# Attention with landmark memories and a bilinear feed-forward: the softmax of four of eight batches moved onto token partitions

## The chip, the cores and the metric

The kernel runs on one core of a Trainium2 chip. The metric is the device time of one execution in microseconds (us), taken as the median of several executions. TensorE is called PE in the profile, its weight loads PEld, VectorE is DVE, ScalarE is ACT, GpSimd is POOL and SyncE is SP.

## The reference, cut to what matters

There are 8 batches, 8 heads, 576 tokens (S), a head size of 64 (D) and 32 memories per head (M). The feed-forward has 512 inputs and 1536 hidden units.

```python
a   = softmax(phi, axis=2)                  # over the tokens
k_m = einsum('bhsm,bhsd->bhmd', a, k)
v_m = einsum('bhsm,bhsd->bhmd', a, v)
scores = matmul(q, k_m.T) / sqrt(64)        # 576 x 32 per head
attn   = softmax(scores, axis=-1)           # over the 32 memories of a head
x   = matmul(attn, v_m)                     # then heads side by side: 4608 x 512
out = ((x @ w_a) * (x @ w_b)) @ w_out       # 4608 x 512
```

The second softmax, over the 32 memories, is what the change moves.

## The kernel before, in words

**The work of one batch.** `exp_phi` (ACT) gives the exponentials of phi. `kv_sums` (PE, tile `pkv`) sums keys, values and a column of ones over the tokens; `take_kv` (DVE) divides by the sum and lays the result out in `rep`; `rep` is transposed into `kvT`, either by PE and a DVE copy (`kv_transpose`, unit `kvt`) or by a DMA transpose that SP issues (`kv_turn`, unit `kvd`). `q_transpose` (DVE) turns the queries into `qT`. `scores` (unit `sc`) multiplies `kvT` and `qT` on PE into four PSUM banks `pscore`, with the 128 (head, memory) pairs of a group g on the partitions and tokens in the columns. `exp_scores` (ACT, L310) writes `E`.

**The normalisation before.** A sum over 32 memories is a sum over partitions there. `denominators` (L320, L321) therefore multiplies `E` by a block matrix `ones` on PE into `pD`, two matmuls of 288 columns per group, and takes the logarithm on ACT (`L`). `normalise` (L329, L331) takes `R` = exp(-L) on ACT and multiplies `E` by `R` into the attention tile `A`, on DVE in batches 0 and 1 and on POOL from batch 2.

**The feed-forward.** The value memories are folded into the weights: `fold` (unit `v0` to `v2`, L343) makes `vab`, one third of 512 hidden units at a time for w_a and w_b (two bodies z), in four PSUM banks `pva`; `take_fold` (units `x0a` and so on, L355) evicts them, group 0 on ACT and group 1 on DVE. `up_half` (L601, L609, L612) multiplies `vab` by `A` in halves of 288 tokens: `pa` is copied to `a_sb` by ACT, and DVE multiplies `a_sb` by `pb` into `ht`. The down projection runs over pairs of 128-token blocks with seven products in place of eight (`two_downs`, L473, tiles `py`, `pv`, `px`); it needs sums of blocks of `ht` that POOL makes (`h_sums`, L455), and its partial results are read by ACT (L480, L527) and DVE (L484).

**The order.** The program's order is written by hand. A batch from the third on has 24 steps (12 blocks of hidden units for each half of the tokens). After each step `work.advance()` issues some down products at an even rate, and then one slot of a side list runs; the side list prepares the next batch. A slot is a set of units joined by `+`; a name with `'` belongs to the batch after that one, `dN` pulls N down products, `L` issues the four loads of two batches later from POOL, `-` does nothing. The lists are `second` (beside batch 2, preparing 3), `every` (beside batches 3, 4 and 5, preparing 4, 5 and 6) and `last` (beside batch 6, preparing 7). Batch 2 is prepared beside the second half of batch 1, by the list `slots(2, ...)` at L699.

**PSUM.** The eight banks are dealt out in a fixed rotation by the class `Banks`: a bank goes to the end of the line when it is taken and again when it is freed. The rotation is decided when the program is written, so PE waits for the very bank that is next in line, even where another is empty. From batch 3 on `work.settle()` finishes the product under way before `sc` and before a pair of folds, so that only the bank of `py` stays held there.

Each engine runs its instructions in the program's order.

Of the kernel before, what the change touches and what calls it, by code (L numbers as in the profile page):

```python
# [8 lines left out]
F32 = mybir.dt.float32  # L9
F16 = mybir.dt.float16  # L10
AF = mybir.ActivationFunctionType
ALU = mybir.AluOpType

P = 128
# [4 lines left out]
def kernel(  # L19
# [11 lines left out]
    nc = tc.nc  # L31

    B, H, S, D = q.shape
    M = phi.shape[3]
# [11 lines left out]
    mid = ctx.enter_context(tc.tile_pool(name="mid", bufs=2))  # L46
    small = ctx.enter_context(tc.tile_pool(name="small", bufs=2))
# [28 lines left out]
    def load_phi(b):  # L76
        phis[b] = inp.tile([P, NHP, NI * M], F32, name="phi_sb")
        nc.gpsimd.dma_start(out=phis[b], in_=rows(phi, b))

    def load_k(b, hps=slice(0, NHP)):  # L80
        kvs[b] = kv_sbs[b % 2]
        nc.gpsimd.dma_start(out=kvs[b][:, 0, hps], in_=rows(k, b)[:, hps])

    def load_v(b, hps=slice(0, NHP)):
        nc.gpsimd.dma_start(out=kvs[b][:, 1, hps], in_=rows(v, b)[:, hps])

    def load_q(b, hps=slice(0, NHP)):
        if b not in qs:
            qs[b] = inp.tile([P, NHP, NI * D], F16, name="q_sb")
        nc.gpsimd.dma_start(out=qs[b][:, hps], in_=rows(q, b)[:, hps])  # L90

    def load(b):
        load_phi(b)
        load_k(b)
        load_v(b)
        load_q(b)
# [81 lines left out]
    attn = {}  # L178
# [7 lines left out]
    def units(b):  # L186

        u = {}
        t = {}
# [133 lines left out]
        def normalise(g, hfs=slice(0, 2)):  # L323
            if g == 0 and hfs.start == 0:
                attn[b] = mid.tile([P, 2, S], F16, name="A")
            sl = slice(HALF * hfs.start, HALF * hfs.stop)
            if hfs.start == 0:
                t["R", g] = small.tile([P, S], F16, name="R")
            nc.scalar.activation(out=t["R", g][:, sl], in_=t["L", g][:, sl], func=AF.Exp, scale=-1.0)  # L329
            engine = nc.vector if b < 2 else nc.gpsimd  # L330
            engine.tensor_tensor(out=attn[b][:, g, sl], in0=t["E"][:, g, sl], in1=t["R", g][:, sl], op=ALU.mult)  # L331

        def fold(lo, hi, zs):
            if b not in vabs:
                vabs[b] = [mid.tile([P, 2, d_ff], F16, name=f"vab{x}") for x in range(2)]
            if len(zs) > 1 and b > 2:
                work.settle()
            for z in zs:
                t["pva", lo, z] = [banks.take([P, 512], F32, "pva", hold=True) for _ in range(2)]
                for j in range(4):  # L340
                    for g in range(2):
                        r, hp = head(g, j)
                        nc.tensor.matmul(  # L343
                            t["pva", lo, z][g][0][32 * j:32 * j + 32, 0:hi - lo],
                            t["kvT"][64 * r:64 * r + 64, 4 + g, M * j:M * j + M],
                            w_sbs[z][64 * r:64 * r + 64, hp, lo:hi],
                            start=True,
                            stop=True,
                            tile_position=(64 * r, 32 * j),
                        )  # L350

        def take_fold(lo, hi, z):
            for g, engine_copy in enumerate((nc.scalar.copy, nc.vector.tensor_copy)):
                pva, bank = t["pva", lo, z][g]
                engine_copy(out=vabs[b][z][:, g, lo:hi], in_=pva[:, 0:hi - lo])  # L355
                banks.free(bank)

        def one(f, *a):
            return lambda: f(*a)

        for z in range(2):
            u[f"exp{z}"] = one(exp_phi, z)
            u[f"ks{z}"] = one(sums, z, 0)
            u[f"kt{z}"] = one(transpose, z, 0)
            u[f"vs{z}"] = one(sums, z, 1)
            u[f"vt{z}"] = one(transpose, z, 1)
            u[f"s{z}"] = one(scores, (z,))
            u[f"e{z}"] = one(exp_scores, z)
            u[f"km{z}"] = one(take_kv, (z,))
            u[f"den{z}"] = one(denominators, z)  # L370
            u[f"nr{z}"] = one(normalise, z)
            for hf in range(2):
                u[f"den{z}{hf}"] = one(denominators, z, (hf,))
                u[f"nr{z}{hf}"] = one(normalise, z, slice(hf, hf + 1))
            for n in range(NCH):
                u[f"v{n}{'ab'[z]}"] = one(fold, 512 * n, 512 * (n + 1), (z,))
                u[f"x{n}{'ab'[z]}"] = one(take_fold, 512 * n, 512 * (n + 1), z)
            for n in range(2):
                u[f"hv{n}{'ab'[z]}"] = one(fold, 256 * n, 256 * (n + 1), (z,))
                u[f"hx{n}{'ab'[z]}"] = one(take_fold, 256 * n, 256 * (n + 1), z)  # L380
# [6 lines left out]
        u["km"] = one(take_kv)  # L387
        u["kvt"] = one(kv_transpose)
        u["kvd"] = one(kv_turn)
        u["-"] = lambda: None  # L390
        return u

# [221 lines left out]
    def up(b, i, hfs):  # L614
        for hf in hfs:
            up_half(b, i, hf, 0)
        if len(hfs) > 1:
            yield
        for hf in hfs:
            up_half(b, i, hf, 1)  # L620
        yield

    def ups(steps, side=()):

        side = iter(side)
        for step in steps:
            for _ in up(*step):
                work.advance()
                next(side, us[step[0]]["-"])()
        for f in side:  # L630
            work.advance()
            f()

    def steps(b, lo, hi):

        return [(b, i, (0, 1)) for i in range(lo, hi)]

    def half_steps(b, hf, lo=0):

        return [(b, i, (hf,)) for i in range(lo, NFF)]  # L640

    us = {b: units(b) for b in range(B)}

    def named(b, names):
# [6 lines left out]
    def slots(b, names):  # L651

        def both(fs):
            return lambda: [f() for f in fs]
        def unit(n):
            if n == "fin":
                return lambda: work.pull(-work.done % NFF)
            if n == "L":
                return lambda: load(b + 2) if b + 2 < B else None
            if n[0] == "y":  # L660
                return lambda: some(int(n[1:]))
            if n[0] == "d" and n[1:].isdigit():
                return lambda: work.pull(int(n[1:]))
            return us[b + n.endswith("'") - n.endswith("_")][n.rstrip("'_")]

        return [both([unit(n) for n in x.split("+")]) for x in names.split()]
# [3 lines left out]
    def some(n):  # L670
        for _ in range(n):
            next(early, None)
# [21 lines left out]
    load(3)  # L694
    sum_weights()
    ups(steps(1, 0, 4), slots(1, "- y1+hv1a+hx1a hv1b+hx1b - y3+v1a+x1a y3+v1b+x1b - -"))
    ups(half_steps(1, 0, 4), slots(1, "- v2a+x2a+v2b+x2b+qt0' - - qt1'+exp0' exp1'+qt2' - kv'+km'+y9"))
    work.plan(S + HALF, 10)
    ups(half_steps(1, 1, 4), slots(2, "qt3 kvt - sc+e0+e1 - den0+den1+nr0 - v0+nr1+x0a x0b - v1+x1b x1a"))  # L699
    second = "v2_+d1+x2a_+exp0 x2b_ exp1 - kv+km+d2 qt0 d4+kvt+qt1 - qt2+qt3+sc+e0 - e1+v0+d2+x0a+x0b den0+d3 exp0' v1+nr0+x1a x1b+qt0' L+d5 den1 v2+x2a exp1'+qt1'+x2b - - qt2'+kv'+nr1+km' - - qt3'+kvt'+d5"  # L700
    every = "- sc+e0 e1 den0 nr0+v0+x0a+x0b - - exp0' exp1' - v1+x1b+x1a+kv'+km0'+d3 - den1+km1' kvd'+qt0' - - nr1+qt1' v2+x2a+x2b - qt2' - qt3' - - L"
    last = "sc+e0 d3 - e1 v0+x0b - - den1 - - den0+d1 x0a+v1+x1b x1a+nr0 - - - v2+x2a - nr1 - - - - x2b"
    for b in range(2, B):
        if b == 2:
            load(4)
        names = second if b == 2 else every if b + 2 < B else last
        side = slots(b + 1, names) if b + 1 < B else []
        for hf in range(2):
            work.plan(S * b + HALF * hf, NFF)
            ups(half_steps(b, hf), side[NFF * hf:NFF * (hf + 1)] if hf == 0 else side[NFF:])  # L710
# [30 lines left out]
```

The softmax here doesn't subtract the row's maximum and nothing guards it: scores larger than these inputs give would overflow.

## Time and profile before

| | |
|---|---|
| median of 5 runs | 241.35 us (241.06 to 241.97) |
| the profiled execution | 241.26 us, of which its span is 239.6 us |
| PE busy | 230.2 us, 96% of the span, 3092 matmuls |
| DVE, ACT, POOL busy | 165.4, 158.5 and 159.3 us |
| granted PE clock | 1.0 |
| normalisation on PE: `pD` | 32 matmuls of 288 columns, four per batch |
| `E`, `L`, `R` on ACT | 419 ns, 426 ns, 712 ns each |
| `A` on POOL | 12 of 1277 ns |
| fold evictions of 512 columns | 44 on ACT at 606 ns, 44 on DVE at 684 ns |
| DMA transposes of `rep` (6 blocks of 128 x 128) | 3, landed 2.7, 3.2 and 3.6 us after issue |

A row of the groups names the line, engine and operation, the tiles written and read, the shape, the count, the busy time and the mean of one. Matmuls overlap in the pipe, so a row's 286 ns for a 288-column matmul is not what the matmul costs; the distance between the starts of two rows in the timeline is.

### The profile page before, as it was taken

What the parts mean: (1) busy time and instruction counts of PE and PEld (TensorE: products, weight loads), DVE (VectorE), ACT (ScalarE), POOL (GpSimd) and SP (SyncE); (2) the same over time, 40 slices, a digit from 0 to 9 for tenths busy, and PEclk for the clock granted to TensorE, in tenths of its full rate; (3) what the DMA queues carried; (4) which work ended last, traced back from release to release, by engine and by line L of the source; (5) the groups of instructions that cost most, each with busy time, mean ns of one, the idle gap of its engine ahead of it and who ended that gap; (6) DMA issues with size and microseconds to landing.
All of it is one profiled execution on the core that took longest, in us unless ns stands there. A gap on an engine that the chain in (4) does not pass through costs nothing.

```text
span 239.6 us, 7764 instructions
## 1 busy us (share of the span) xinstructions
PE 230.2 (96%) x3092; PEld 170.0 (71%) x3092; DVE 165.4 (69%) x403; ACT 158.5 (66%) x410; POOL 159.3 (66%) x135
## 2 busy tenths in 40 slices
PE   7968999999999999999999999999999999999993
PEld 7634664446757867878787787878787778888882
DVE  4636783469949878976974659775976585756642
ACT  2267671669698599687776857697776877465330
POOL 7953244499979639981799948984769087936001
PEclk9999999999999999999999999999999999999999
DMA  6999999999967954992359945599230303032154
GB/s 237 238 195 206 207 258 205 254 211 280 223 151 164 208 118 97 228 204 48 47 120 232 211 91 68 150 199 193 45 81 15 77 19 72 11 82 63 39 129 122
DMA packets 28164, 34.71 MB, mean 145 GB/s; under 512 B 4416, under 2 KB 22208, under 8 KB 28128
## 3 DMA queue, kind: packets, MB, share of 16 engines
q0 software_dynamic: 19264, 23.14, 52.1%
q1 hardware_dynamic: 8352, 10.29, 18.2%
q10 hardware_dynamic: 512, 0.79, 1.0%
q8 instruction: 24, 0.39, 0.6%
q14 instruction: 12, 0.10, 0.1%
HBM read 42.47 MB, written 9.44 MB: 217 GB/s over the span
## 4 chain that ended last, share of the span: by engine, by line
PE 76%; DMA 16%; DVE 2%; ACT 2%; issue 1%; POOL 1%; DVEq 0%; POOLq 0%
PE py L473 18%; PE pa L601 17%; PE pb L601 16%; PE pv L473 9%; DMA wb_sb<-in_moe_w_b_dram 6%; DMA q_sb<-in_q_dram 5%; PE pva L343 5%; DMA kv_sb<-in_v_dram 4%; PE px L473 4%; PE po L398 2%; PE pkv L212 2%; PE pscore L297 1%; PE pD L320 1%; ACT a_sb L609 1%; DVE ht L612 1%
## 5 line engine op out<-in xcount | busy, mean ns | idle before, releaser
L612 DVE TENSOR_TENSOR ht<-a_sb,pb 128x288 f16<-128x288 f16 x168 | 73.2, 449 | 37.5 <-ACT a_sb L609 28.4
L601 PEld LDWEIGHTS <-vab 128*128 128x128 f16 x768 | 72.4, 98 | 25.0 <-issue 7.9
L609 ACT CAST a_sb<-pa 128x288 f16<-128x288 f32 x168 | 66.8, 408 | 25.8 <-PE pa L601 24.6
L601 PE MATMUL pa<-A,vab 128*128 128x288 f16 x384 | 75.8, 287 | 0.1
L601 PE MATMUL pb<-A,vab 128*128 128x288 f16 x384 | 74.9, 286 | 0.7 <-ACT vab L355 0.5
L455 POOL TENSOR_TENSOR h_sums<-ht 128x768 f16<-128x768 f16 x28 | 46.0, 1643 | 33.9 <-DVE ht L612 33.8
L473 PEld LDWEIGHTS <-h_sums 128*128 128x128 f16 x384 | 37.0, 98 | 7.7 <-issue 1.1
L355 DVE CAST vab<-pva 128x512 f16<-128x512 f32 (+1 forms) x52 | 32.3, 644 | 4.8 <-PE pva L343 4.2
L355 ACT CAST vab<-pva 128x512 f16<-128x512 f32 (+1 forms) x52 | 27.8, 572 | 7.8 <-PE pva L343 7.4
L473 PEld LDWEIGHTS <-ht 128*128 128x128 f16 x288 | 28.1, 98 | 5.7 <-issue 0.4
L473 PE MATMUL py<-w_sums,h_sums 128*128 128x256 f16 x192 | 31.3, 273 | 0.0
L455 POOL TENSOR_TENSOR h_sums<-h_sums,ht 128x768 f16<-128x768 f16 x14 | 22.9, 1639 | 1.0
L455 POOL TENSOR_TENSOR h_sums<-ht,h_sums 128x768 f16<-128x768 f16 x14 | 23.0, 1642 | 0.9
L310 ACT ACTIVATE E<-pscore 128x288 f16<-128x288 f32 x32 | 11.4, 419 | 11.5 <-PE pscore L297 11.4
L331 POOL TENSOR_TENSOR A<-E,R 128x576 f16<-128x576 f16 x12 | 15.3, 1277 | 4.3 <-ACT R L329 4.3
L473 PE MATMUL py<-wo_sb,ht 128*128 128x256 f16 x96 | 16.7, 273 | 0.0
L473 PE MATMUL pv<-w_sums,h_sums 128*128 128x256 f16 x96 | 16.5, 273 | 0.0
L473 PE MATMUL py<-w_sums,ht 128*128 128x256 f16 x96 | 15.9, 272 | 0.1
L473 PE MATMUL px<-wo_sb,ht 128*128 128x256 f16 x96 | 15.9, 273 | 0.0
L321 ACT ACTIVATE L<-pD 128x288 f32<-128x288 f32 x32 | 11.6, 426 | 5.8 <-PE pD L320 5.6
L480 ACT ACTIVATE u<-py 128x256 f32<-128x256 f32 x32 | 12.5, 391 | 4.3 <-PE py L473 3.7
L203 DVE STREAM_TRANSPOSE qT<-q_sb 128x288 f32<-128x288 f32 x32 | 14.5, 464 | 0.5 <-DMA q_sb<-in_q_dram 0.4
(65 smaller groups left out, 274.9 us busy)
## 6 DMA issues: line engine op xcount, KB each, us to landing
out_dram<-o_sb SPq DMA_DIRECT2D x68, 128.0 KB, 2.4
phi_sb<-in_phi_dram POOLq DMA_DIRECT2D x8, 576.0 KB, 5.3
kv_sb<-in_v_dram POOLq DMA_DIRECT2D x7, 576.0 KB, 10.5
kv_sb<-in_k_dram POOLq DMA_DIRECT2D x7, 576.0 KB, 6.9
q_sb<-in_q_dram POOLq DMA_DIRECT2D x6, 576.0 KB, 13.4
wo_sb<-in_moe_w_out_dram POOLq DMA_DIRECT2D x6, 256.0 KB, 13.9
q_sb<-in_q_dram POOLq DMA_DIRECT2D x4, 288.0 KB, 9.7
wa_sb<-in_moe_w_a_dram POOLq DMA_DIRECT2D x2, 512.0 KB, 13.7
```

The lines of the kernel that those rows point to most:

```text
L203: nc.vector.transpose(out=t["qT"][:, hp, :].bitcast(F32), in_=qs[b][:, hp, :].bitcast(F32))
L310: nc.scalar.activation(out=Ev[:, g, :, z, :], in_=pss, func=AF.Exp, scale=1.0 / (8.0 * CS))
L321: nc.scalar.activation(out=t["L", g][:, sl], in_=pD, func=AF.Ln)
L331: engine.tensor_tensor(out=attn[b][:, g, sl], in0=t["E"][:, g, sl], in1=t["R", g][:, sl], op=ALU.mult)
L343: nc.tensor.matmul(t["pva", lo, z][g][0][32 * j:32 * j + 32, 0:hi - lo], t["kvT"][64 * r:64 * r + 64, 4 + g, M * j:M * j + M], w_sbs[z][64 ...
L355: engine_copy(out=vabs[b][z][:, g, lo:hi], in_=pva[:, 0:hi - lo])
L455: engine.tensor_tensor(out=out, in0=in0, in1=in1, op=op)
L473: nc.tensor.matmul(po, lhs[:, i], rhs[:, i], start=first and i == 0, stop=i == KH - 1, skip_group_check=not first)
L480: nc.scalar.mul(out=x, in_=po, mul=scale)
L601: nc.tensor.matmul(ps, vabs[b][x][:, g, P * i:P * (i + 1)], attn[b][:, g, HALF * hf:HALF * (hf + 1)], start=(g == 0), stop=(g == 1))
L609: nc.scalar.copy(out=a_sbs[b, i, hf], in_=ps)
L612: nc.vector.tensor_tensor(out=ht[:, i, t0:t0 + HALF], in0=a_sbs.pop((b, i, hf)), in1=ps, op=ALU.mult)
```

## The change

In batches 4 to 7 the tile `E` is turned by a DMA transpose on SP so that tokens lie on the partitions (`e_turn`, nine blocks of 128 x 128). DVE sums the 32 memories along the free dimension and takes the reciprocals (`token_sums`, in two parts of 20 and 16 sums). The product with the reciprocals is written in place, five blocks on POOL and four on DVE (`token_normalise`). A second DMA transpose on SP writes `A` (`a_turn`). `denominators` and `normalise` are no longer called for these batches. Batch 2 normalises on DVE. In batches 4 to 7 the two evictions of the middle third that were on DVE go to ACT, eight instructions in all. The memories of batch 4 are turned by DMA (`kvd'`) where PE and DVE did it before (the one `kvt'` that goes). Queries are turned on VectorE in both kernels. The four side lists are written anew, and the loads of a batch (`L`) stand at other places.

```diff
-            engine = nc.vector if b < 2 else nc.gpsimd
+            engine = nc.vector if b < 3 else nc.gpsimd
             engine.tensor_tensor(out=attn[b][:, g, sl], in0=t["E"][:, g, sl], in1=t["R", g][:, sl], op=ALU.mult)
+
+        def e_turn():
+            t["ET"] = mid.tile([P, 2, S], F16, name="E").rearrange("p g s -> p (g s)").rearrange("p (n x) -> p n x", x=P)
+            nc.sync.dma_start_transpose(out=t["ET"], in_=t["E"].rearrange("p g s -> p (g s)"))
+
+        def blocks(x):
+            return t["ET"][:, slice(0, 5) if x == 0 else slice(5, 9)].rearrange("p n (j m) -> p (n j) m", m=M)
+
+        def token_sums(x):
+            if x == 0:
+                t["sum"] = small.tile([P, 36], F32, name="sum")
+            out = t["sum"][:, slice(0, 20) if x == 0 else slice(20, 36)]
+            nc.vector.tensor_reduce(out=out, in_=blocks(x), axis=mybir.AxisListType.X, op=ALU.add)
+            nc.vector.reciprocal(out=out, in_=out)
+
+        def token_normalise(x):
+            sums = t["sum"][:, slice(0, 20) if x == 0 else slice(20, 36)]
+            engine = (nc.gpsimd, nc.vector)[x]
+            engine.tensor_tensor(out=blocks(x), in0=blocks(x), in1=sums.unsqueeze(2).to_broadcast(list(blocks(x).shape)),
+                                 op=ALU.mult)
+
+        def a_turn():
+            attn[b] = mid.tile([P, 2, S], F16, name="A")
+            nc.sync.dma_start_transpose(out=attn[b].rearrange("p g s -> p (g s)").rearrange("p (n x) -> p n x", x=P),
+                                        in_=t["ET"].rearrange("p n x -> p (n x)"))
...
-            for g, engine_copy in enumerate((nc.scalar.copy, nc.vector.tensor_copy)):
+            copies = (nc.scalar.copy, nc.scalar.copy if b > 3 and lo == 512 else nc.vector.tensor_copy)
+            for g, engine_copy in enumerate(copies):
...
+        u["ed"] = e_turn
+        for x in range(2):
+            u[f"sm{x}"] = one(token_sums, x)
+            u[f"tn{x}"] = one(token_normalise, x)
+        u["ad"] = a_turn
...
-    ups(half_steps(1, 0, 4), slots(1, "- v2a+x2a+v2b+x2b+qt0' - - qt1'+exp0' exp1'+qt2' - kv'+km'+y9"))
+    ups(half_steps(1, 0, 4), slots(1, "- v2a+x2a+v2b+x2b - qt0' qt1'+exp0' exp1'+qt2' - kv'+km'+y9"))
...
-    ups(half_steps(1, 1, 4), slots(2, "qt3 kvt - sc+e0+e1 - den0+den1+nr0 - v0+nr1+x0a x0b - v1+x1b x1a"))
-    second = "v2_+d1+x2a_+exp0 x2b_ exp1 - kv+km+d2 qt0 d4+kvt+qt1 - qt2+qt3+sc+e0 - e1+v0+d2+x0a+x0b den0+d3 exp0' v1+nr0+x1a x1b+qt0' L+d5 den1 v2+x2a exp1'+qt1'+x2b - - qt2'+kv'+nr1+km' - - qt3'+kvt'+d5"
-    every = "- sc+e0 e1 den0 nr0+v0+x0a+x0b - - exp0' exp1' - v1+x1b+x1a+kv'+km0'+d3 - den1+km1' kvd'+qt0' - - nr1+qt1' v2+x2a+x2b - qt2' - qt3' - - L"
-    last = "sc+e0 d3 - e1 v0+x0b - - den1 - - den0+d1 x0a+v1+x1b x1a+nr0 - - - v2+x2a - nr1 - - - - x2b"
+    ups(half_steps(1, 1, 4), slots(2, "qt3 kvt - sc+e0+e1+den0+den1+nr0 - - L v0+nr1+x0b - - d4+v1+x0a+x1a+x1b d1"))
+    second = "v2_+d2+x2a_+x2b_+exp0 - exp1 - kv+km+d2 qt0 d4+qt1+kvt qt2 L+d1+qt3+sc+e0 - d2+v0+e1+x0a+x0b - den0+exp0'+d2 v1+nr0+x1a x1b+d10+exp1' - qt0' v2+x2a+x2b+kv' - den1+km0' km1'+kvd' nr1+qt1' qt2' qt3' - d6"
+    every = "exp0' sc+exp1'+e0+e1+v0+x0a+x0b+d3+ed - kv'+km0' km1' - sm0 sm1+tn0+kvd' - tn1+d2 d3 v1+qt0'+x1a+ad d3+L+x1b qt1' - qt2' - v2+x2a+x2b - qt3' - - - - -"
+    last = "sc e0+e1+ed - v0+x0b - - sm0 x0a+sm1+tn0 d2+v1+d3+x1b+tn1 - ad+d6 x1a - - - - v2+x2a - - - - - x2b"
     for b in range(2, B):
-        if b == 2:
-            load(4)
```

## The prediction

> **What bounds the kernel now.** I read the page's engine shares first, then the clock row and the chain.
>
> ```profile
> PE 230.2 (96%) x3092; PEld 170.0 (71%) x3092; DVE 165.4 (69%) x403; ACT 158.5 (66%) x410; POOL 159.3 (66%) x135
> ...
> PE   7968999999999999999999999999999999999993
> ...
> PEclk9999999999999999999999999999999999999999
> ...
> PE 76%; DMA 16%; DVE 2%; ACT 2%; issue 1%; POOL 1%; DVEq 0%; POOLq 0%
> ```
>
> PE is full in every slice from the fifth on, at full clock, and the chain's DMA share lies before 42 us, ahead of anything the change touches. So a batch costs what PE issues plus what PE waits. A busy share does not show waits, because matmuls overlap; the distance between starts does. The timeline of PE, ACT and DVE beside batch 4 shows both:
>
> ```profile
> 127.21 0.47 PE L297 MATMUL pscore<-qT,kvT 32*32 32x288 f16 x32
> ...
> 127.61 0.42 PE L601 MATMUL pa<-A,vab 128*128 128x288 f16 x2
> 127.70 0.71 ACT L310 ACTIVATE E<-pscore 128x288 f16<-128x288 f32 x2 [1.32 <-PE pscore L297]
> 127.87 0.41 PE L601 MATMUL pb<-A,vab 128*128 128x288 f16 x2
> ...
> 128.80 0.41 PE L601 MATMUL pb<-A,vab 128*128 128x288 f16 x2
> ...
> 129.64 0.45 DVE L612 TENSOR_TENSOR ht<-a_sb,pb 128x288 f16<-128x288 f16 x1 [0.46 <-ACT a_sb L609]
> ...
> 129.81 0.41 PE L320 MATMUL pD<-E,ones 128*128 128x288 f16 x2
> 130.05 0.41 PE L601 MATMUL pa<-A,vab 128*128 128x288 f16 x2
> ...
> 132.87 0.41 PE L343 MATMUL pva<-wa_sb,kvT 64*32 64x512 f16 x8
> ...
> 133.10 0.40 PE L343 MATMUL pva<-wb_sb,kvT 64*32 64x512 f16 x8
> ...
> 133.43 0.42 PE L601 MATMUL pa<-A,vab 128*128 128x288 f16 x2
> ```
>
> The reader takes four prices from it: a pair of `pD` costs PE 0.24 us (129.81 to 130.05); PE is free 0.40 us after the scores begin, while the first `E` starts after 0.49; a second fold follows the first by 0.23 and leaves PE 0.33 later; `ht` starts about 0.85 after its `pb`. Steps (`pa`, `pb`) cost 0.49, a down product 0.11. Only PE time counts; ACT, for one, spends 24.6 us waiting for `pa`.
>
> **What the change takes off PE.** Eight pairs of `pD` go (batches 4 to 7): 8 x 0.24 = 1.94 us. Batch 4's six PE transposes go; the chain gives one set 0.33. Together 2.27 us, in a stretch where PE has no slack, so all of it counts unless PE waits instead.
>
> **What it takes off and adds elsewhere.** ACT, per batch: minus 4 x 426 and 2 x 712 ns, plus two evictions of 606, net minus 1.9 us; worth nothing by itself. POOL loses two of 1277 ns a batch and gains one of five blocks, 1277 x 640/576 = 1.42 us; its operand is broadcast and 32-bit, which no row shows, so 1.37 (the `h_sums` rate) to twice that. `h_sums` are asked for 24 products ahead, 2.6 us of products plus some six steps of 0.49, which hides either. DVE gains two sums over 640 and 512 elements, two reciprocals (161 ns) and a product of 512, and loses two evictions of 684. No row shows a reduction. The nearest are the eviction (one input, 32-bit on one side, 1.34 ns per element) and `h_sums` on DVE (549 ns for 768, 0.71): 0.46 to 0.86 and 0.37 to 0.68 us; I take 1.2 ns, nearer the eviction: 0.77 and 0.61, and 0.62 for the product. DVE: 2.3 minus 1.4, plus 0.95 a batch, on an engine that is 69% busy. Batch 2's two products on DVE are 2 x 0.46, priced with the start below.
>
> The Trainium skill ("VectorE: DVE Perf Modes", rules for kernel authors) calls `tensor_reduce` the slowest DVE operation and says to expect one element a cycle; no run here shows it yet.
>
> **The DMA transposes.** The tile view of `kvT` has the only rows:
>
> ```profile
> L247 SPq DMA_TRANSPOSE kvT<-rep x3: 1212/1222/2055, 116.1 to 170.3; - x3
> ...
> DMA to landing us min/median/max: 2.7/3.2/3.6
> ```
>
> Six blocks land after 3.2 us; nine, in proportion, after 4.8 (2.7 if size costs nothing, 5.4 from the slowest). `A` is needed some eleven steps after `ad`, so the second turn is hidden at any of these. The first is not obviously hidden: `sm0` stands in DVE's queue, and every later `ht` stands behind it. In the list `every`, with S the start of the scores: the four `E` start at S+0.49 and follow each other by 0.30, so the last ends at S+1.8; the turn lands at S+6.7. On PE, folds, three downs, two steps, `pkv`, and three more steps with five downs end near S+5.8, and DVE, with two `take_kv` of 0.9 in that stretch, reaches `sm0` near S+6.6. The two meet. Beyond that there is slack: with `py` and `pv` held, six banks rotate, so PE can be three steps (2.5 us) ahead, of which 0.85 is used: 1.6 us. `sm0` to `tn1` put 2.3 us on DVE within four steps, which eats most of it. Price 0 to 0.4 a batch; I take 0.05, 0.2 in all. SP's queue: `ed` waits for `E` with stores of `o_sb` behind it, up to 2 us; `o_sb` has four buffers and a batch (25.3 us from one scores row, 101.87, to the next) stores 2.25 pairs of blocks, so nobody waits.
>
> The Trainium skill ("VectorE: DVE Perf Modes", the three transpose paths) speaks against the change: 1309 ns for one 128 x 128 block by DMA against 390 by TensorE. Nine blocks one after another would take 11.8 us and land 7 us after DVE gets there; less 1.6 of slack, four batches would lose some 22 us, 262 in all, against 240.7 by the row (an estimate from the page's figure). But by that sum the six blocks above would have taken 7.9 us, and they took 3.2, so the row decides.
>
> **What the new lists add on PE.** (1) In `every`, `v0` follows the scores at once. After settling, `py` holds one bank; scores take four of the other seven; `e0` and `e1` put them back at the end of the line; the folds take the three that remain and then the bank of the first `E`. That `E` ends at S+0.49+0.42 = S+0.91, while PE wants the bank at S+0.40+0.23 = S+0.63: a wait of 0.3 us, in three batches, 0.9. Before, `v0` came several steps later. (2) The ACT queue then holds four `E` and two evictions (0.47 apart), ending at S+2.75; beside batch 3, only three downs and two steps stand before `pkv`, which wants that bank at S+2.6: 0.2 once. Beside 4 and 5 at least seven more downs stand between. (3) `v1` and `pkv` were neighbours; `pva` to `pkv` takes 0.21, `pva` to the next step 0.33: three times 0.1, 0.3.
>
> (4) The start of batch 2:
>
> ```profile
> 65.36 0.63 PE L297 MATMUL pscore<-qT,kvT 32*32 32x288 f16 x32
> 65.84 1.32 ACT L310 ACTIVATE E<-pscore 128x288 f16<-128x288 f32 x4
> 65.92 0.42 PE L601 MATMUL pa<-A,vab 128*128 128x288 f16 x2
> ...
> 69.89 0.89 PE L343 MATMUL pva<-wb_sb,kvT 64*32 64x512 f16 x8
> ```
>
> All four `pD` now stand right behind the scores and wait until `E` ends at 67.16: the next `pa` starts at 67.46, not 65.92. The work that before filled this (two steps, three downs) ends 0.65 later. Part comes back: `L` and `R` are done sooner, and the fold at 69.89, 0.89 long where 0.56 is the rule for a whole pair, waits less. Following the banks with ACT's instructions at the distance of their starts (0.30 for `E`, 0.58 for `R`, 0.28 for a copy), PE reaches batch 2's second step 0.3 late. With the same rows laid end to end it is 1.5 late; if every wait there vanished, 0.4 early. I take 0.3, since the trace shows them overlapping. (5) In batch 3 two downs come between the second step after the scores and `v0`, where a fold pair took 0.89 (85.17 to 86.06) in place of 0.56: minus 0.2.
>
> **The sum.** 241.26 (the profiled execution, 1.7 us outside its span) - 2.27 + 0.9 + 0.2 + 0.3 + 0.3 - 0.2 + 0.2 = 240.7. The median of the runs is 0.09 above the profiled one, which is less than I can resolve; 0.2% (0.48 us) is about what a measurement of this kernel can tell from no change.
>
> **Rivals.** *Full gain.* The waits (1), (2) and DVE's do not come, because banks are free earlier than I count: 241.26 - 2.27 + 0.3 + 0.3 - 0.2 = 239.4. For it: before, PE passes nearly every bank without waiting. Against: the rotation names the very bank.
> *Cancelled.* The start costs 0.9 (between my ends) instead of 0.3: 241.3. For it: ACT has the longest unbroken run of work there.
> *DVE becomes the bound (slower).* The turn lands late or the reduction is dear; `ht` queues behind `sm0`, and `pb` banks run out. It decides from about 1.6 us past S+6.7, that is from a landing near 6.5 us after issue, or sums costing twice what I take; each further us costs four. At a landing of 7.3 us: 0.8 x 4 = 3.2, 243.9. For it: DVE meets the turn with no margin, and the measured turns ran while few bytes moved. Against: the slowest of three scales to 5.4.
>
> **Chances.** Forecast 0.48: 0.36 of it below 240.87, 0.10 within 0.2%, 0.02 above. Full gain 0.20, cancelled 0.10, slower 0.22. So faster 0.56, same 0.20, slower 0.24. The range runs from 239.0, a little under the full gain, to 242.8, inside the slow case, and leaves out one in ten on each side.
>
> **What would show it.** Right: `pD` with 16 matmuls; the second fold after the scores starts some 0.55 after the first, beside batches 3 to 5; first turns landing 4 to 5.4 us after issue, and `ht` waiting little for the DMA. Wrong: DVE idle at `sm0` for over a microsecond, fold pairs after the scores at 0.56 us in all (full gain), or PE starts in the 65 to 76 us stretch over 0.6 late.

## The result, and the profile after

The changed kernel takes 241.85 us (median of 30 runs; 241.61 to 242.43 but for one disturbed run), the kernel before 241.33 us in its runs beside it (53). The ratio is 1.0019 with an interval of 1.0013 to 1.0025: slower by 0.5 us, where 240.7 was forecast. The profiled execution took 241.72 us, with a span of 240.0 us.

From the page of the changed kernel, the engines' busy time and share of the span, and the chain of waits:

```profile
PE 228.0 (95%) x3070; PEld 167.9 (70%) x3070; DVE 170.4 (71%) x416; ACT 153.2 (64%) x394; POOL 152.4 (63%) x129
...
PE 75%; DMA 16%; DVE 2%; POOL 2%; issue 1%; ACT 1%; DVEq 0%; POOLq 0%
```

PE has 22 matmuls and 2.2 us of busy time less, as the sum had it. The kernel is not faster, so PE waits longer somewhere. To find where, I compare the start of the same `pa` step in both traces and correct for down products that were done earlier or later (0.11 us each). That gives a lag of the changed kernel at the start of each batch (0.11 of the first 1.99 stood already at the start of batch 1):

| start of batch | 2 | 3 | 4 | 5 | 6 | 7 | near the end |
|---|---|---|---|---|---|---|---|
| lag, us | +1.99 | +1.29 | +1.35 | +1.19 | +1.13 | +0.65 | +0.64 |
| change since the column before | +1.99 | -0.70 | +0.06 | -0.16 | -0.06 | -0.48 | 0 |
| the prediction's terms for it | +0.3 | -0.53 | +0.16 | -0.04 | -0.04 | -0.44 | 0 |

Only the first column is far off. From batch 2 on the change earns 1.34 us where 0.89 was predicted; all of that, and more, is lost before batch 2 starts. The timeline of that stretch (start, length, engine, line, tiles; in brackets the wait before it):

```profile
65.52 0.54 PE L297 MATMUL pscore<-qT,kvT 32*32 32x288 f16 x32
66.01 1.32 ACT L310 ACTIVATE E<-pscore 128x288 f16<-128x288 f32 x4
66.77 0.41 PE L320 MATMUL pD<-E,ones 128*128 128x288 f16 x2 [0.72 <-ACT E L310]
...
67.62 0.41 PE L632 MATMUL pa<-A,vab 128*128 128x288 f16 x2
...
69.13 0.46 DVE L331 TENSOR_TENSOR A<-E,R 128x576 f16<-128x576 f16 x1 [3.09 <-ACT R L329]
...
71.18 2.17 DVE L331 TENSOR_TENSOR A<-E,R 128x576 f16<-128x576 f16 x1
...
71.38 1.65 POOL L486 TENSOR_TENSOR h_sums<-ht 128x768 f16<-128x768 f16 x1
...
72.43 0.38 PE L368 MATMUL pva<-wb_sb,kvT 64*32 64x512 f16 x1
...
73.11 1.74 POOL L486 TENSOR_TENSOR h_sums<-h_sums,ht 128x768 f16<-128x768 f16 x1
73.28 1.87 DVE L381 CAST vab<-pva 128x512 f16<-128x512 f32 x3
...
74.01 0.41 PE L368 MATMUL pva<-wb_sb,kvT 64*32 64x512 f16 x7 [1.21 <-DVE vab L381]
```

Up to 71.1 us this is the predicted course: `pa` returns 2.10 after the scores (predicted 67.46 minus 65.36, the same 2.10). Then two rows of one line and one shape differ: the first product of batch 2 takes 0.46 us, the second 2.17. Beside the second, POOL runs `h_sums`, a product with two operands in SBUF like DVE's own; the DVE product ends at 73.35, soon after the first POOL product has ended (73.03). The evictions of the fold stand behind it on DVE, so `pva` finds no bank: one matmul at 72.43 and the other seven 1.58 us later. That is the loss. In the kernel before, these two products were POOL's own work, so POOL could not run `h_sums` beside them, and no row of its trace shows a DVE product of two SBUF operands beside a product of POOL. That both operands lie in SBUF seems to be what matters: in the changed kernel 84 `ht` products, which read `pb` from PSUM, overlap a `h_sums` of POOL and take 0.40 to 0.46 us, as they do without it.

The trace has a second, smaller instance, later, where it hides behind other work:

```profile
139.53 1.64 POOL L486 TENSOR_TENSOR h_sums<-ht,h_sums 128x768 f16<-128x768 f16 x1
140.66 1.05 DVE L350 TENSOR_TENSOR E<-E,sum 128x512 f16<-128x512 f16 x1
...
141.12 2.09 POOL L486 TENSOR_TENSOR h_sums<-ht 128x768 f16<-128x768 f16 x1
```

Both engines lose here: DVE takes 1.05 (the median of this row is 0.68), the next POOL product 2.09 (1.64 elsewhere). The same pair comes back in all eleven runs below that have the turned softmax, at 1.04 to 1.06 and 2.08 to 2.09.

The new steps themselves, in the tile view of `E` (min, median, max in ns, first and last start):

```profile
L344 DVE TENSOR_REDUCE sum<-E x8: 673/743/812, 110.5 to 189.1; 128x20 f32<-128x640 f16 x4, 128x16 f32<-128x512 f16 x4
L335 SPq DMA_TRANSPOSE E<-E x4: 1310/1406/1728, 105.8 to 183.2; - x4
L350 POOL TENSOR_TENSOR E<-E,sum x4: 1262/1263/1265, 111.7 to 188.4; 128x640 f16<-128x640 f16 x4
L350 DVE TENSOR_TENSOR E<-E,sum x4: 681/685/1051, 113.4 to 190.8; 128x512 f16<-128x512 f16 x4
...
DMA to landing us min/median/max: 3.2/3.2/4.1
```

The sums take 0.81 and 0.67 us (0.77 and 0.61 were taken), the products 1.26 on POOL and 0.68 on DVE (1.42 and 0.62). The turn of nine blocks lands after 3.2 to 4.1 us, hardly later than six blocks did before (2.7 to 3.6) and far from half as long again.

### The profile page after: what moved, and what is told of

It is laid out like the page before. It is cut to its first block, busy times and chain, and to the rows that moved or that the text cites. A ratio compares the mean times of both kernels' runs of the same rounds, so it can differ in the third digit from the quotient of the medians.

```text
span 240.0 us, 7733 instructions
## 1 busy us (share of the span) xinstructions
PE 228.0 (95%) x3070; PEld 167.9 (70%) x3070; DVE 170.4 (71%) x416; ACT 153.2 (64%) x394; POOL 152.4 (63%) x129
## 4 chain that ended last, share of the span: by engine, by line
PE 75%; DMA 16%; DVE 2%; POOL 2%; issue 1%; ACT 1%; DVEq 0%; POOLq 0%
PE pa L632 18%; PE py L504 17%; PE pb L632 17%; PE pv L504 9%; DMA phi_sb<-in_phi_dram 6%; PE pva L368 5%; DMA wo_sb<-in_moe_w_out_dram 5%; DMA wa_sb<-in_moe_w_a_dram 5%; PE px L504 4%; PE pkv L212 2%; PE po L429 2%; PE pscore L297 1%; DVE A L331 1%; ACT E L310 1%; POOL q_sb L90 0%
## 5 line engine op out<-in xcount | busy, mean ns | idle before, releaser
L643 DVE TENSOR_TENSOR ht<-a_sb,pb 128x288 f16<-128x288 f16 x168 | 72.0, 445 | 31.9 <-ACT a_sb L640 23.8
L640 ACT CAST a_sb<-pa 128x288 f16<-128x288 f32 x168 | 65.5, 411 | 30.9 <-PE pa L632 29.5
L381 ACT CAST vab<-pva 128x512 f16<-128x512 f32 (+1 forms) x60 | 32.0, 575 | 9.2 <-PE pva L368 9.1
L504 PE MATMUL py<-w_sums,h_sums 128*128 128x256 f16 x192 | 30.6, 273 | 0.0
L381 DVE CAST vab<-pva 128x512 f16<-128x512 f32 (+1 forms) x44 | 26.9, 636 | 5.3 <-PE pva L368 5.2
L504 PE MATMUL py<-wo_sb,ht 128*128 128x256 f16 x96 | 15.9, 273 | 0.0
L504 PE MATMUL pv<-w_sums,h_sums 128*128 128x256 f16 x96 | 15.9, 273 | 0.0
L504 PE MATMUL px<-wo_sb,ht 128*128 128x256 f16 x96 | 15.2, 273 | 0.0
L194 ACT ACTIVATE exp_sb<-phi_sb 128x576 f16<-128x576 f32 x16 | 10.8, 688 | 5.4 <-DMA phi_sb<-in_phi_dram 5.4
L504 PE MATMUL pv<-wo_sb,h_sums 128*128 128x256 f16 x96 | 14.2, 273 | 0.0
```

Of the source, the lines that this page charges most:

```text
L194: nc.scalar.activation(out=t["exp"][:, 2 * z:2 * z + 2, :, :], in_=phis[b][:, 2 * z:2 * z + 2, :].rearrange("p c (i m) -> p c i m", m=M), ...
L504: nc.tensor.matmul(po, lhs[:, i], rhs[:, i], start=first and i == 0, stop=i == KH - 1, skip_group_check=not first)
L640: nc.scalar.copy(out=a_sbs[b, i, hf], in_=ps)
L643: nc.vector.tensor_tensor(out=ht[:, i, t0:t0 + HALF], in0=a_sbs.pop((b, i, hf)), in1=ps, op=ALU.mult)
```

## The experiments

*Theory:* the loss is the DVE product held by POOL's product; all else is as predicted or better. *Rivals:* the new start costs by itself (PE waits for `E` at `pD`, the cancelled case); or the softmax of batches 4 to 7 gains nothing.

**POOL held off.** POOL copies eight columns of the finished product first, so its `h_sums` starts behind it; nothing else changes.

```diff
 engine.tensor_tensor(out=attn[b][:, g, sl], in0=t["E"][:, g, sl], in1=t["R", g][:, sl], op=ALU.mult)
+if b == 2 and g == 1:
+    t["seen"] = small.tile([P, 8], F16, name="seen")
+    nc.gpsimd.tensor_copy(out=t["seen"], in_=attn[b][:, 1, 0:8])
```

> The changed kernel, with one small POOL copy that reads the last product of batch 2's softmax, so that the POOL sums behind it start only when that DVE product is done. Theory (the DVE product of two 16-bit SBUF tensors cannot run beside a POOL product and waited for it): the product takes 0.46 us instead of 2.17, PE's wait of 1.55 us in the fold behind it falls to 0.2 or less, and the time falls by 1.4 us, to about 240.4. Rival A (the product is slow in itself, or because POOL issues loads): it stays near 2.2 us and the time near 241.85. Rival B (the four denominators right behind the scores are the cost): the time falls by less than 0.4 us.

Measured: 240.05 us (239.97 to 240.29), ratio to the kernel before 0.9944 [0.9932, 0.9957]. The timeline:

```profile
71.03 0.46 DVE L331 TENSOR_TENSOR A<-E,R 128x576 f16<-128x576 f16 x1
...
71.55 0.19 POOL L334 COPY seen<-A 128x8 f16<-128x8 f16 x1 [0.34 <-DVE A L331]
71.70 1.63 POOL L489 TENSOR_TENSOR h_sums<-ht 128x768 f16<-128x768 f16 x1
```

The product takes 0.46 again, the fold no longer breaks, and the lag at the start of batch 2 is +0.24, beside the predicted 0.3. One copy of eight columns is worth 1.8 us.

**The start of before.** The list of batch 2's preparation, the engine of its products and the place of `load(4)` as they were.

```diff
-    ups(..., slots(2, "qt3 kvt - sc+e0+e1+den0+den1+nr0 - - L v0+nr1+x0b - - d4+v1+x0a+x1a+x1b d1"))
+    ups(..., slots(2, "qt3 kvt - sc+e0+e1 - den0+den1+nr0 - v0+nr1+x0a x0b - v1+x1b x1a"))
-            engine = nc.vector if b < 3 else nc.gpsimd
+            engine = nc.vector if b < 2 else nc.gpsimd
...
+        if b == 2:
+            load(4)
```

> The changed kernel with the preparation of batch 2 as it was before (its side list, its products on POOL, the loads of batch 4 at their old place). Theory (the start loses 2.0 us, the rest of the change gains 1.3): about 239.9 us. Rival (the DMA transposes and the lists of batches 4 to 7 are what eats the gain): 241.2 us or more.

Measured: 240.05 us (239.74 to 240.74), 0.9947 [0.9932, 0.9962]. So the rest of the change, the softmax by DMA with its lists and evictions, does gain 1.25 us, and the new start, freed of its stall, is worth no more than the old one.

**The new start alone**, those three edits the other way round in the kernel before.

> The kernel before with only the new preparation of batch 2 (new side list, products on DVE, loads of batch 4 earlier). Theory: the product of 2.2 us and the 1.4 us in front of the denominators appear here too; 2.0 us slower than before, about 243.3 us. Rival (the loss comes from the new list beside batch 2 or later): 241.3 to 241.8 us.

Measured: 243.17 us, 1.0074 [1.0061, 1.0087]. Its trace has no transposed softmax, and its second product takes 2.18 us, from 71.08, with `h_sums` beginning at 71.27. The lag is 1.89 at the start of batch 2 and 1.95 at the end: this loss is never won back.

**A copy in its place.** POOL copies 768 columns, one operand, ahead of the `h_sums` that met the product, into a quarter that `h_sums` overwrites later.

```diff
+        if len(h_sums) == 2:
+            engine.tensor_copy(out=t[3], in_=a11)
```

> The kernel after with one POOL copy of 128x768 (one input) ahead of the POOL product that ran beside the 2.17 us DVE product, so that POOL is copying while DVE multiplies. It computes the same. If the DVE product was held by a POOL operation with two inputs, the copy leaves it at 0.46 us, the product of POOL starts after it, and the time is that of the kernel with POOL held: 240.0 to 240.3. Rival: any POOL operation on the same memory holds it; then the DVE product takes about 0.2 us plus the length of the copy plus what is left of itself, 1.2 to 1.9 us in all, and the time is 240.9 to 241.9.

Measured: 240.49 us (240.22 to 241.58), 0.9971 [0.9955, 0.9987].

```profile
71.20 0.44 DVE L331 TENSOR_TENSOR A<-E,R 128x576 f16<-128x576 f16 x1
71.35 0.97 POOL L485 COPY h_sums<-ht 128x768 f16<-128x768 f16 x1
72.30 1.63 POOL L488 TENSOR_TENSOR h_sums<-ht 128x768 f16<-128x768 f16 x1
```

POOL begins at nearly the same distance behind the DVE product as before (0.15 us against 0.20), but with one operand, and the product is not held. The time is 0.2 us above the range that was expected for this. Whether the copy in turn waited was still open.

**Two copies** behind each other, the second beside evictions that read PSUM.

> The run with one POOL copy of 128x768 ahead of the POOL product left open whether the copy stands beside the DVE product freely or merely waited for it: the copy began 0.15 us after the DVE product and took 0.97 us, and no row shows how long such a copy takes by itself. Here two such copies follow each other; the second runs beside evictions of DVE, which read PSUM. If both take 0.97, the copy and the DVE product do not hold each other; if the second takes about 0.7 (0.97 less the 0.3 that the two overlapped), the copy waited and one operand is enough. The DVE product takes 0.46 by either. The time is that of the run with one copy, 240.5, or up to 0.3 more, since h_sums starts one copy later and is wanted much later.

Measured: 240.41 us (240.33 to 240.49), 0.9955 [0.9939, 0.9971]. The tile view:

```profile
L486 POOL COPY h_sums<-ht x2: 827/898/970, 71.3 to 72.3; 128x768 f16<-128x768 f16 x2
```

The two take 1.86 together, 0.97 and then 0.83. The first is 0.14 longer, half of the 0.30 that it overlaps the product, so this lies between the two expectations and decides nothing. Left open too is why batch 2's *first* product took 0.69 to 0.70 us in these two runs (0.46 elsewhere); PE's fold began 0.23 later for it, and that is about half of what these runs stand above 240.05.

**The folds two slots later.** Beside batches 3 to 5 the pair of folds `v0`, the second of which waits behind the scores, goes two slots later, into the slot of `kv'`, to get that wait back. (Some of the expectations call this the second fold and one slot.)

```diff
-    every = "exp0' sc+exp1'+e0+e1+v0+x0a+x0b+d3+ed - kv'+km0' km1' - ...
+    every = "exp0' sc+exp1'+e0+e1+d3+ed - v0+x0a+x0b+kv'+km0' km1' - ...
```

> The changed kernel with the first fold of batches 4 to 6 moved from right behind the scores to two steps later, in front of the sums of keys and values. Theory (PE waits 0.3 us for the bank of the first E in each of the three, and the neighbours fold and sums save 0.1 more): second fold 0.23 us after the first, 1.2 us less, about 240.65 us. Rival (PE waits for the same evictions at the new place): within 0.3 us of 241.85.

Measured: 241.42 us (241.11 to 242.41), 1.0007 [0.9996, 1.0019]: 0.43 below the changed kernel, not 1.2. Batch by batch, the change of the lag is -0.58 beside 4 (the changed kernel: -0.16, so 0.42 gained). Beside 3 nothing is gained (+0.09), for PE now waits 0.44 between the fold and `pkv` instead. Beside 5, in the profiled execution, the lag grows by 0.59. There DVE waits for the turn:

```profile
158.20 1.33 SPq L335 DMA_TRANSPOSE E<-E  x1
...
159.68 4.90 SPq L493 DMA_DIRECT2D out_dram<-o_sb  x4
...
164.75 0.82 DVE L344 TENSOR_REDUCE sum<-E 128x20 f32<-128x640 f16 x1 [1.11 <-DMA E<-E]
```

Four stores follow the turn in SP's queue, the first after 1.5 us (4 us in the changed kernel), and it lands 6.5 us after its issue instead of 3.2 to 4.1. That the stores delay it is not shown by itself: in other runs a turn with its first store 1.4 to 2.3 us behind it landed after 3.2 to 5.5 us. This is the rival in which DVE becomes the bound, in small. The profiled execution took 242.04 us, 0.6 above the median, which suggests that the landing is not as late in most executions; batch 4's 0.42 is about what the median shows.

**Both: the start of before and the folds later.**

> The kernel after with the start of before, and with the second fold one slot later in the list of batches 3 to 5. If the two losses add up, the start gives back 1.80 (as it did alone: 240.05) and the fold 0.43 (as it did alone: 241.42 against 241.85): 239.6. The fold's 0.43 was made of 0.6 gained beside batch 4, nothing beside batch 3 (PE waits 0.44 ahead of pkv instead) and 0.6 lost beside batch 5, where the turn landed 6.5 us after its issue with four stores queued 1.3 us behind it. If that late landing is a matter of where the stores happen to fall, the shift of 1.8 us at the start does not change it, because turn and stores shift together: again 6.5 us and 239.6. Rival: it was chance of one execution; then the turn lands after 3.2 to 4.1 us and the time is 239.0.

Measured: 239.89 us (239.34 to 240.21), 0.9932 [0.9915, 0.995]. The turn beside batch 5 landed after 5.5 us; PE gained 0.44 at the fold and lost 0.33 at `pa` and `pkv`. The landing lies between the two expectations; the time is above both (239.6 and 239.0).

**The `pD` two slots later**, with POOL held and the folds later beside batch 4 alone. In this list the loads `L` and the folds of batch 2 move one slot later as well.

```diff
-    slots(2, "qt3 kvt - sc+e0+e1+den0+den1+nr0 - - L v0+nr1+x0b - - ...
+    slots(2, "qt3 kvt - sc+e0+e1 - den0+den1+nr0 - L v0+nr1+x0b - - ...
```

> The kernel with POOL held behind the product (240.05), the four pD of batch 2 one slot later, and the second fold one slot later beside batch 4 alone. Beside batch 4 the fold gives 0.6 as in the run with the fold later: 239.5 by itself. The pD: if the wait of PE for E behind the scores of batch 2 (0.72 and 0.20 in the trace) is won back within the start, as the prediction had it, moving them gives at most the 0.24 by which that start is late: 239.2 to 239.5. Rival (the cancelled case of the prediction): the wait is lost for good and the start stays late by another wait otherwise; then 0.7 to 0.9 more comes back and the time is 238.6 to 238.8.

Measured: 240.24 us (240.14 to 240.78), 0.9956 [0.9942, 0.9971], slower than either expectation. PE no longer waits for `E` behind the scores (0.81 and 0.37 between starts with POOL held alone), but it waits at the folds behind (0.36 inside the first pair), and by the fourth step of batch 2 the start is 0.6 late instead of 0.23 (counted from batch 1, as this execution was 0.62 late before that). So the wait for `E` was won back within the start, as the prediction had it, and this list, which takes it away, costs.

**The same without the later `pD`.**

> The kernel with POOL held behind the product (240.05) and the second fold one slot later beside batch 4 alone, without the later pD of the run that had both (240.24). By the trace of that run the later pD cost about 0.4 at the start and another 0.15 on the way, and the fold gave 0.59: 240.05 - 0.59 = 239.5, the same as with the start of before and this fold (239.47). Rival: the later pD were not what cost, and the two edits just do not add; then 240.1 to 240.3 again.

Measured: 239.76 us (239.62 to 240.51), 0.9929 [0.9914, 0.9945]. The 0.48 comes back, so the list with the later `pD` was what cost. The expectation was 0.26 too low, and 0.16 of that because it counted 0.59 for the folds, the whole change of the lag beside batch 4; 0.16 of that change is the changed kernel's own, and the folds' part is 0.43.

**A list for each of batches 3, 4 and 5**, on the start of before.

```diff
+    beside = {3: "exp0' sc+exp1'+e0+e1+d3+ed - v0+x0a+x0b kv'+km0' km1' sm0 ...",
+              4: "exp0' sc+exp1'+e0+e1+d3+ed - v0+x0a+x0b+kv'+km0' km1' - sm0 ...",
+              5: "exp0' sc+exp1'+e0+e1+ed - v0+x0a+x0b+d3+kv'+km0' km1' - sm0 ..."}
```

> The kernel after with the start of before (240.05) and the second fold moved one slot later beside batches 3, 4 and 5, each with its own list: beside 3 kv' and km0' move one slot later too, so that pkv does not come right behind the fold; beside 5 d3 moves behind the fold, so that its stores come after the turn has landed. The folds behind the scores cost PE 0.44 us of pva a batch in the trace (2.00 instead of 1.56). If each list gives its 0.44 back: 240.05 - 1.3 = 238.7. If only batch 4 does and the other two keep a wait of the same size at pkv or at the turn, as with one list for all: 239.5.

Measured: 239.72 us (239.33 to 240.59), 0.9929 [0.9911, 0.9946]. Only batch 4's list paid. Beside 3 the folds cost 2.01 us in `pva` again, now ahead of a step. Beside 5 the stores still came 1.8 us behind the turn, and `pa` took 0.43 more.

**The folds later beside batch 4 alone**, on the start of before.

> The kernel after with the start of before (240.05) and the second fold one slot later beside batch 4 alone, where it gave 0.43 to 0.59 in two runs: 239.5 to 239.6.

Measured: 239.47 us (239.43 to 239.67), 0.9915 [0.9899, 0.993]. In the traces the folds' new place gives 0.43 over the run with the start of before; the medians differ by 0.58. This version beats both kernels, the one before by 1.9 us and the changed one by 2.4.

**The turn behind two more stores** in SP's queue, on the start of before.

```diff
-    every = "exp0' sc+exp1'+e0+e1+v0+x0a+x0b+d3+ed - kv'+km0' km1' - sm0 ...
+    every = "exp0' sc+exp1'+e0+e1+v0+x0a+x0b+d3 - kv'+km0' km1' ed sm0 ...
-    last = "sc e0+e1+ed - v0+x0b - - sm0 ...
+    last = "sc e0+e1 - v0+x0b ed - sm0 ...
```

> The kernel after with the start of before (240.05), and the first DMA transpose of each batch later in the queue of SP, behind two stores that it stood ahead of. Those stores end at 108.6 beside batch 3, 131.6 beside 4, about 162.0 beside 5 and 184.2 beside the last, and the turn lands 3.2 us later: 111.9, 134.8, 165.2 and 187.4. DVE comes to its first sum at 108.6, 135.2, 163.4 and 187.2 in the run with the start of before. So DVE would wait 3.3 us in batch 4 of the preparation and 1.8 in batch 6, and next to nothing in 5 and 7. With the 1.6 us of slack that the prediction gave PE, the loss is 1.7 + 0.2: 241.9. Rival: no slack is left, since ht stands behind the sums and PE has its banks full: 5.1 us, 245.2. Second rival: DVE catches up by itself: 240.1.

Measured: 249.07 us (248.55 to 250.24), 1.032 [1.0293, 1.0346], above all three expectations. Its timeline in the preparation of batch 4:

```profile
108.48 1.33 SPq L335 DMA_TRANSPOSE E<-E  x1
...
111.91 0.82 DVE L344 TENSOR_REDUCE sum<-E 128x20 f32<-128x640 f16 x1 [3.52 <-DMA E<-E]
...
113.41 0.41 PE L632 MATMUL pb<-A,vab 128*128 128x288 f16 x2 [2.85 <-DVE ht L643]
```

DVE waits 3.52 us (3.3 was expected). PE has some cover, and its wait at `pb` is 2.85; but the batch loses 4.9 us in all. The likely reason is that the sums, reciprocals and products that then stand ahead of `ht` are no longer done in idle time; no run separates them. Beside batch 5 the turn went out at 166.50, not 162: it queues behind stores that wait for down products not yet done. DVE waited 8.7 us in three batches (3.52, 2.94 and 2.21), which by the lag, less that of the run with the start of before, lost 4.8, 2.5 and 1.4 us; the kernel lost 9.0.

## Why the prediction was wrong, point by point

**What bounds the kernel: right.** PE, its issue time plus its waits. Everything below is a term of that sum.

**The gain on PE: right.** The price of `pD` came out to the hundredth (8 x 0.24 is 1.92, though, not 1.94): in the whole of batch 4's steps the distances between PE's starts add up like this, before and after.

| us | `pD` | `pva` | `pv` | all the rest | sum |
|---|---|---|---|---|---|
| before | 0.49 | 1.56 | 4.28 | 23.10 | 29.43 |
| after | 0 | 2.00 | 4.02 | 23.25 | 29.27 |

The transposes beside batch 2 fall from 0.67 to 0.34, so batch 4's six took 0.33, as priced.

**Waits (1) and (3): right in mechanism and size.** `pva` costs 0.44 more (0.3 + 0.1 predicted) beside 3, 4 and 5. The timeline beside batch 4:

```profile
128.56 0.47 PE L297 MATMUL pscore<-qT,kvT 32*32 32x288 f16 x32
...
128.96 0.41 PE L368 MATMUL pva<-wa_sb,kvT 64*32 64x512 f16 x8
129.19 0.73 PE L368 MATMUL pva<-wb_sb,kvT 64*32 64x512 f16 x8
...
129.85 0.50 PE L504 MATMUL py<-w_sums,ht 128*128 128x256 f16 x3
```

The second fold begins 0.23 behind the first, not 0.55: three banks are free, and the wait of 0.30 stands inside its row, ahead of the fourth. The reader of a row's length (0.73, where 0.40 is the rule) sees it; a look at starts alone misses it.

**Wait (2), term (5) and DVE: too dear.** `pkv` costs 0.1 beside batch 3 (0.2). Beside `second` PE gains 0.70 (0.53), and beside batch 4 `pv` takes 0.26 less, which had no term. DVE's 0.2 was nothing. Beside batch 3 DVE comes to the first sum at S+6.65 (110.47 minus 103.82), as reckoned, but the turn has landed at S+5.2 (issued at 105.76, landed 3.2 later), not S+6.7. Beside batch 4 DVE comes only at S+8.5 (137.10 minus 128.56), and the turn lands at S+5.6 (130.39 plus 3.8).

**Term (4), the start of batch 2: this step failed.** "Batch 2's two products on DVE are 2 x 0.46, priced with the start below" is where. One took 0.46, the other 2.17, and the start came 1.99 late instead of 0.3. The reckoning of banks and ACT around it was sound: with the product at 0.46 again the start is 0.24 late, and with that one term mended the kernel takes 240.05, which is 0.65 below the forecast mostly because the terms above were too dear. (One reading in it was loose: the 0.89 at 69.89 is the row of one fold, not of a pair; the pair took 1.08 where 0.56 is the rule.) The 0.46 came from two rows of batch 1, at 43.21 and 47.28, where POOL was not multiplying. The change did two things at once there: it gave the products to DVE and thereby freed POOL to run `h_sums` beside them. That `h_sums` met the second product and not the first came from the loads `L`, which now stand ahead of it on POOL and end at 71.37. The sign that the prediction had set for this, PE starts over 0.6 late between 65 and 76 us, came.

The Trainium skill states a rule for this ("SBUF — State Buffer", section "SBUF: two separate sides"): a VectorE instruction with two SBUF inputs and a GpSimd instruction that reads SBUF take one pair of ports, as an exclusive lock, which the first to start holds to its end. The prediction did not weigh it. The rows agree that the two exclude each other (2.17 for 0.46; 1.05 and 2.09 for 0.68 and 1.64). By the starts that the profile records they do not agree that the first to start wins, for at 71.18 DVE started 0.20 ahead of POOL and still lost. The copy of one operand neither confirms nor refutes the rule: it began behind the product, which kept its 0.44, and whether it waited stayed open (0.97 against 0.83). The measurement decides: such a pair costs what the rows show, in whichever order the trace has them.

**The rivals.** The cancelled case had the right place, but half the size (start 0.9 late where 1.99 was measured) and not the cause: ACT's run of work and the wait at `pD` were won back; that its 241.3 lies near the 241.85 is luck. The full gain did not come, since waits (1) and (3) did; 239.47, near its 239.4, was reached by moving one of them away and not by banks that came free earlier. DVE as the bound did not occur in the changed kernel. Its point of decision was too late: at a landing of 6.5 us the slack of 1.6 should just have been used up, and one batch lost 1.1 (the lag's 0.65 above the changed kernel's own, and the 0.44 that the folds gave), as much as DVE waited. Its price, one us of PE for each of DVE, held in the sum of the three batches with the late turn (8.7 for 8.7), though not in each of them (4.8 for 3.5, 2.5 for 2.9, 1.4 for 2.2).

## What to carry to other kernels

When an operation moves from one engine to another, ask what the engine that is now free will do at that very time, and whether the trace of before has a row with both running together; if it has none, the duration from a quiet row is a lower bound. A VectorE product of two SBUF operands beside a two-operand GpSimd product is such a pair, and a copy of a few columns that orders one behind the other can be worth far more than it costs. Taking away a wait pays only where nothing else meets the same bank or queue: the same edit paid beside one batch of three.

## What the hardware showed that was not expected

A DVE product of 576 columns took 2.17 and 2.18 us instead of 0.46, in all three kernels in which POOL's product of two operands began 0.2 us behind it (the changed one, the new start alone and the first with a later fold), and 0.44 to 0.46 in five runs where POOL began later or with a copy. A DMA transpose of nine blocks landed after 3.2 us in the median of the changed kernel's eight, as six blocks did before; one with four stores from 1.5 us behind it took 6.5, and the cause of that is open. The reciprocals of 20 and 16 values took 0.25 to 0.28 us, where one value takes 0.16.
